# Transposes of seven late bursts on two engines, and another order of four readers of PSUM

## The chip, the cores and the metric

The kernel runs on one core of a Trainium2 chip. The metric is the device time of one execution in microseconds (us). The engines are TensorE (PE, with its weight loads PEld), VectorE (DVE), ScalarE (ACT), GpSimd (POOL) and SyncE (SP, which issues DMAs).

## The reference

Attention within chunks of 64 rows, over 8 batches, 8 heads and 576 rows of 64, then a feed-forward layer with softplus over the 4608 resulting rows:

```
scores = matmul(q_c, k_c^T) / sqrt(64)            # per chunk of 64 rows
attn   = exp(scores - max) ; attn /= sum(attn) + 1e-9
x      = (attn @ v_c), heads side by side          # 4608 x 512
h      = x @ w_in                                  # 512 x 2048
g      = max(h, 0) + log1p(exp(-|h|))              # softplus
out    = g @ w_out                                 # 2048 x 512
```

All in float32.

## The kernel before

**The work.** The rows are cut into 36 attention blocks of 128 rows (two chunks) and 9 row tiles of 512 rows for the feed-forward layer. Every float32 matrix product is made of three matmuls: a high part of each operand (rounded copy) and a low part (the difference), as high x high, low x high and high x low.

**The stages.** Row tiles 0 to 2 are done in the plain way, up to about 315 us. Then come three "super pairs" of two row tiles each. In a super pair the products with `w_in` are made in seven products P0 to P6 instead of eight, by sums of blocks; `pairs` holds eight steps of each super pair, called pairs here. In a pair, PE runs P1, P2, P0, P3, one product with `w_out` for the pair before (12 matmuls), P4, P5, P6, and another such product; then the next pair's P1. Each P has six matmuls. In the second half of super pairs 0 and 1 PE does only products with `w_out`. The third super pair (in `BOTH`) uses sums for `w_out` as well, so its pairs have two short products (`R1`, `R0`) of six matmuls there. 

**The banks.** `pa_tile()` gives a PSUM tile of two banks; there are two such tiles. In `product`, one tile holds banks 1 and 2 of the pair, the other banks 0 and 3. Readers of a pair: `hold` (s0, s1, s2) copies banks 0, 1, 2 out on ACT (L792). `mix` (L805) makes sums: `d` and `c22` on POOL, the others on DVE: `e` reads bank 3, `f` reads bank 1, `f2` reads bank 2, `c11` reads bank 0. `soft` (L816; L814 in the third super pair) applies softplus on ACT: `soft10` reads bank 1, `soft01` reads bank 2, `soft11` and `soft00` read sums in SBUF. The next pair's P1 takes the tile of banks 1 and 2, after `soft10`, `soft01` and `f2`.

**The bursts.** Attention of blocks 4 to 35 runs in bursts (`burst`): 64 small matmuls each for values and scores of two blocks. After a burst come, for each of its two blocks, maximum and subtraction (DVE), exp on ACT (with a table load of its own), the sum of exp (DVE), a normalization on DVE or POOL (L595), and the transposition of the exp values within each chunk, which the next burst needs as `eT`. The code uses VectorE's transpose on squares of 32x32 (`BL`), each transposed in its place. For blocks in `SWAP_DVE`, `blk_e4` makes eight transposes of a quarter of the partitions (L544): `Tf` is the first four, `Te` the other four. They read `qe` and write `eT`. For other blocks one whole transpose `blk_e` (L532) goes from `qe` to `ka`, and DMAs then move the squares across partitions. Blocks 22 to 35 belong to seven late bursts, in super pairs 0 and 1 (from about 357 us on). In super pairs 0 and 1 a burst stands in pairs 2, 5 and 7 and once in the second half.

**The order.** `Plan` decides the order of all instructions of each engine. It goes forward in time with a cost for each task, and starts on each free engine the ready task of lowest `urg` (then the one added first). A result counts as ready for another engine 0.15 us after its end (`CROSS`) and for the same engine 0.08 us after it (`OWN`). A task with `urg` of 0 or more isn't started when a task with negative `urg` on that engine is due within 0.5 us (`HOLD`). A change of ACT's function table between exp and softplus counts 1.28 us. The readers above have negative `urg`; the transposes have `urg=d`, which is positive. The order found is written out, the engines run their instructions in that order, and the waits between engines come from the framework, which tracks which tile is read and written.

Costs of the planner that matter here: P 1.36, product with `w_out` 2.72, `hold` 0.59, `mix` on DVE 0.69, softplus 0.60, normalization on DVE 0.65.

Of the kernel before, what the change touches and what calls it, by code (L numbers as in the profile page):

```python
# [33 lines left out]
class Plan:  # L34


    CROSS = 0.15
# [123 lines left out]
def chunked_attention_softplus_ffn(  # L161
# [9 lines left out]
    nc = tc.nc  # L171
# [4 lines left out]
    BL = 32  # L176
# [6 lines left out]
    NPT = B * NCH // 2  # L183
# [69 lines left out]
    live = {}  # L253
# [280 lines left out]
    def blk_et(i):  # L534
        return blk_tile("eT").rearrange("p (u h k) -> p u h k", u=2, h=H)

    def blk_e4(i, a):
# [7 lines left out]
        if a == 1:  # L545
            live.pop(("e", i)), live.pop(("eA", i))

    def blk_swap(i):
        ea = live.pop(("eA", i))
        eT = blk_et(i)  # L550
        for a in range(2):
            for kb in range(2):
                for tb in range(2):
                    d, s = (2 * a + kb) * BL, (2 * a + tb) * BL
                    (nc.scalar if i in SWAP_ACT else nc.sync).dma_start(eT[d : d + BL, tb], ea[s : s + BL, kb])
        live["eT", i] = eT
# [494 lines left out]
    WHOLE = (4, 5, 9)  # L1051
    SWAP_DVE = (4, 7, 9, 10, 11, 13, 14, 15, 16, 17, 19, 20, 21, 22, 23, 24, 25, 26, 27, 28, 29, 30, 31, 32, 33, 34, 35)
    SWAP_ACT = ()
    BEGIN = (4, 8, 15)
    BURST_AT = (22, 26, 32, 36, 40, 44)
    HOMES = {(n, i): ("early", 2 * (i - FIRST_BLK) + j) for i in (5, 7) for j, n in enumerate("qk")}
# [91 lines left out]
    for u, (g, is_in, fc) in enumerate(units):  # L1148
        (of_in if is_in else of_out)[fc] = u
        d = due(g) - 4  # L1150
        last = [f"w_hi{u}", f"w_lo{u}"]
        users = []
        if not is_in and fc >= HALF_FC:
            for j in range(2 * (fc - HALF_FC), min(2 * (fc - HALF_FC) + 2, LATE)):
# [11 lines left out]
                 urg=d, take=[("top", [f"w_add{u}"])])  # L1166
# [131 lines left out]
    for key, (pv, ps) in bursts.items():  # L1298
# [40 lines left out]
        for n in range(2):  # L1339
            i = a + n  # L1340
            plan.add(f"v{i}", LOADER.get(("v", i), "SP"), 2.4, partial(blk_v_load, i), free_of["v", i], urg=d + V_LATE if ("v", i) in HOMES else d - V_URG, kb=310, parts=4,
                     after=[V_AFTER])
            first = [f"B{at}_{n}"] if bursts[key][0] is None else [f"xh{2 * bursts[key][0] + n}"]
            plan.add(f"max{i}", "DVE", 0.68, partial(att_max, i), first, urg=d + 0.2 * n if key in BEGIN else n - 5,
                     after=[f"sub{a}"] if n else [])
            plan.add(f"sub{i}", "DVE", 0.68, partial(att_sub, i), [f"max{i}"], urg=d + 0.2 * n if key in BEGIN else n - 5)
            plan.add(f"exp{i}", "ACT", 0.62, partial(att_exp, i), [f"sub{b}"], urg=d if key in BEGIN else -6, table="exp",
                     after=[f"hi{at + 1}"] if at in BEGIN else [])
            plan.add(f"den{i}", "DVE", 1.25, partial(att_den, i), [f"exp{i}"], urg=d)
            pool = i in NORM_POOL  # L1350
            plan.add(f"norm{i}", "POOL" if pool else "DVE", 1.05 if pool else 0.65, partial(att_norm, i),
                     [f"den{i}"], urg=d)
            gone = [f"V{FIRST_BLK - 1}"] if ps == F else [f"B{at}_{n}"]
            if i in SWAP_DVE:
                plan.add(f"Tf{i}", "DVE", 1.76, partial(blk_e4, i, 0), [f"norm{i}"] + gone, urg=d)
                plan.add(f"Te{i}", "DVE", 1.76, partial(blk_e4, i, 1), [f"Tf{i}"], urg=d)
                swapped[i] = f"Te{i}"
            else:
                plan.add(f"Te{i}", "DVE", 0.65, partial(blk_e, i), [f"norm{i}"], urg=d)
                plan.add(f"swap{i}", "ACT" if i in SWAP_ACT else "SP", 4.8, partial(blk_swap, i), [f"Te{i}"] + gone, urg=d - SW_URG, kb=190, parts=8)  # L1360
                swapped[i] = f"swap{i}"
# [55 lines left out]
    for at, w in enumerate(pairs):  # L1417
        n, j, name = w["s"], w["j"], w["name"]
        d = due((n, 0, j)) - 9
        for part in range(2):  # L1420
            needs = [] if at > 1 else [f"G1_{FAST * FC - 1}"]
            if not at and not part:
                needs = [f"B{BURST_AT[-1]}_{i}" for i in range(2)]
            if n == 0:
                needs += [f"wd{j}_{i}" for i in range(3)] + own
            if n in BOTH and j % 2:
                needs += [f"x{q}{n}_{k}" for q in "HL" for k in range(7)]
            plan.add(f"ring{part}_{name}", QUEUE["ring"], ISSUE[QUEUE["ring"]], partial(ring_load, w, part), needs, urg=d - 20, kb=660 if part else 880,
                     take=[(("ring", "other")[n in BOTH and j % 2] + str(part), [f"P{6 if part else 3}_{name}"])] if at or part else [],
                     after=[f"ring{part}_{pairs[at - 1]['name']}"] if at else [])  # L1430
        for k in range(7):
            needs = [f"ring{k // NX}_{name}", f"xH{n}_{k}", f"xL{n}_{k}"]
            needs += [before[f"P{k}_{name}"]] + {4: [f"s1_{name}"], 5: [f"s2_{name}"], 6: [f"s0_{name}", f"e_{name}"]}.get(k, [])
            take = []
            if k == ORDER[0]:
                take = [("pa", [f"soft10_{name}", f"soft01_{name}", f"f2_{name}"])]
            elif k == ORDER[2]:
                take = [("pa", [f"c11_{name}", f"e_{name}"])]
            plan.add(f"P{k}_{name}", "PE", PM, partial(product, w, k), needs, urg=1e6, take=take)
        for q in range(3):  # L1440
            past = [f"{t}_{pairs[at - 1]['name']}" for t in (("soft11",), ("c22", "f"), ("d",))[q]] if at else []
            plan.add(f"s{q}_{name}", "ACT", 0.59, partial(hold, w, q), [f"P{q}_{name}"] + past, urg=-3 if n in BOTH else -2)
        for what, needs in (
            ("d", ["s1", "s2"]), ("e", ["s0", "P3"]), ("c22", ["e", "d"]), ("f", ["d", "P5"]), ("f2", ["f", "P5"]),
            ("c11", ["f2", "P6"]),
        ):
            pool = what in MIX_POOL
            past = [f"soft00_{pairs[at - 1]['name']}"] if at and what == "f" else []
            plan.add(f"{what}_{name}", "POOL" if pool else "DVE", 1.3 if pool else 0.69, partial(mix, w, what),
                     [f"{t}_{name}" for t in needs] + past, urg=-2)  # L1450
        a, b = (v_["name"] for v_ in w["first"])
        for i, jj, what in ((1, 0, "P5"), (0, 1, "P5"), (1, 1, "c22"), (0, 0, "c11")):
            kept = [f"lo{v_['name']}" for v_ in w["second"]] if j == FC // 2 - 1 else [f"us{name}"]
            take = {(1, 0): [("uu0", [f"lo{a}", f"lo{b}"])], (0, 1): [("uu1", kept)]}.get((i, jj), [])
            needs = [f"{what}_{name}"] + {(0, 0): [f"soft10_{name}"], (1, 1): [f"soft01_{name}"]}.get((i, jj), [])
            if n in BOTH:
                take = []
                if j > 1:
                    needs += [f"R{i}_{j - 2}", f"vt{j - 2}_{i}"] + [f"own{j - 2}{q}" for q in range(2)] * i
                elif j:  # L1460
                    needs += [f"B{tag(list(bursts)[-1])}_{b}" for b in range(2)]
                else:
                    needs += [f"lo{v_['name']}" for w_ in pairs[at - FC // 2 : at] for v_ in w_["second"]]
            plan.add(f"soft{i}{jj}_{name}", "ACT", 0.6, partial(soft, w, i, jj), needs, urg=-2, table="softplus", take=take)
        if n in BOTH:
            continue
        if j < FC // 2 - 1:
            plan.add(f"us{name}", QUEUE["us"], ISSUE[QUEUE["us"]], partial(spill_store, w), [f"soft01_{name}", f"soft11_{name}"], urg=-1, kb=400)
            a, b = (v_["name"] for v_ in w["second"])
            plan.add(f"ul{name}", QUEUE["ul"], ISSUE[QUEUE["ul"]], partial(spill_load, w), [f"us{name}", f"soft{1 - j % 2}{j % 2}_{n}_{FC // 2 - 1}"],  # L1470
                     urg=due((n, 1, 2 * j + 2)) - 12, kb=400,
                     take=[(f"uu{j % 2}", [f"lo{a}", f"lo{b}"])], after=[f"ul{n}_{j - 1}"] if j else [])
        for group in ("first", "second"):
            for i in (1, 0) if group == "first" else (0, 1):
                v_ = w[group][i]
                b = v_["name"]
                src = f"ul{name}" if group == "second" and j < FC // 2 - 1 else f"soft{i}{int(group == 'second')}_{name}"
                plan.add(f"hi{b}", "ACT", 0.62, partial(sp_hi, v_), [src], urg=-1, take=[("g", [f"G2_{b}"])],
                         after=[f"hi{w[group][1]['name']}"] if group == "first" and i == 0 else [])
                plan.add(f"lo{b}", "DVE", 0.69, partial(sp_lo, v_, False), [f"hi{b}"], urg=-1)  # L1480
# [198 lines left out]
```

## Time and profile before

| | |
|---|---|
| median of 3 runs | 832.38 us (832.22 to 832.39) |
| profiled execution, its own time | 831.0 us |
| its span, first to last instruction | 829.2 us |
| PE busy | 809.3 us, 98% of the span |
| DVE, ACT, POOL busy | 583.3, 403.1, 406.9 us |

The span is the profiled execution without what lies around it. Busy time is the union of an engine's instructions; waiting of the engine's sequencer isn't in it. Matmuls overlap, so the busy share of PE counts a pipelined stretch as full.

### The profile page before, as it was taken

Reading aid. Unit: us, or ns where it says so; the run is one execution under the profiler, and the core shown is the slowest. Engines: PE = TensorE matmul, PEld = TensorE weight load, DVE = VectorE, ACT = ScalarE, POOL = GpSimd, SP = SyncE. Lnnn points to the kernel's source line nnn. Section 1 sums busy time; section 2 is a strip of 40 time slices with the busy share of each in tenths; the row PEclk is TensorE's granted clock in tenths of the full one; section 3 lists DMA queues with packets and bytes.
Section 4 is the critical chain, followed back from the end, with each engine's and each line's share of the span. In section 5 each row is a group of like instructions: output and inputs, shape, how many; then the busy total and the mean of one; then the engine's idle time right before and its main releaser. Section 6 shows DMA issues by size and latency. Waiting matters only on the chain.

```text
span 829.2 us, 15528 instructions
## 1 busy us (share of the span) xinstructions
PE 809.3 (98%) x5675; PEld 664.0 (80%) x5675; DVE 583.3 (70%) x938; ACT 403.1 (49%) x664; POOL 406.9 (49%) x467
## 2 busy tenths in 40 slices
PE   8799999999999999999999999999999999999997
PEld 7688778888887888888888888888887787878886
DVE  4898987087478777667487888483878935555984
ACT  3767764345344564344434434434454644454551
POOL 1457659879975822322334212132188539972213
PEclk9899999999999999999999999999999999999999
DMA  9977758644674454776749536859558565666563
GB/s 207 251 181 201 188 174 238 199 111 123 152 199 112 112 145 153 226 214 180 205 164 225 151 105 205 230 162 233 158 149 269 190 228 187 208 218 212 158 208 68
DMA packets 202877, 151.27 MB, mean 182 GB/s; under 512 B 161136, under 2 KB 176752, under 8 KB 198576
## 3 DMA queue, kind: packets, MB, share of 16 engines
q1 hardware_dynamic: 189424, 99.66, 44.6%
q0 software_dynamic: 11232, 50.34, 19.8%
q8 instruction: 45, 0.74, 0.4%
q10 hardware_dynamic: 2144, 0.26, 0.2%
q14 instruction: 32, 0.26, 0.1%
HBM read 106.95 MB, written 41.94 MB: 180 GB/s over the span
## 4 chain that ended last, share of the span: by engine, by line
PE 74%; DVE 8%; DMA 5%; ACT 4%; POOL 3%; issue 3%; SPq 2%; DVEq 0%; POOLq 0%; ACTq 0%
PE po L1002 29%; PE pa L786 22%; PE pa L644 13%; PE po L938 8%; PE pa L608 2%; DVE wib L805 2%; PE pa L520 1%; DMA raw<-in_moe_w_in_dram 1%; DVE g_lo L660 1%; SPq L359 1%; POOL raw L873 1%; DMA images<-raw 1%; POOL wib L805 1%; DVE eT L544 1%; ACT ends L816 1%
## 5 line engine op out<-in xcount | busy, mean ns | idle before, releaser
L805 POOL TENSOR_TENSOR wib<-wib 128x512 f32<-128x512 f32 x48 | 65.5, 1364 | 180.7 <-ACT wib L792 158.5
L1002 PE MATMUL po<-late,g_hi 128*128 128x512 f32 x420 | 128.8, 392 | 0.0
L786 PE MATMUL pa<-wi_hi,xb 128*128 128x512 f32 x304 | 94.8, 393 | 1.8 <-DVE wib L805 1.1
L544 DVE STREAM_TRANSPOSE eT<-qe 32x256 f32<-32x256 f32 x216 | 93.9, 435 | 3.1
L1002 PEld LDWEIGHTS po<-late,g_hi 128*128 128x128 f32 x420 | 78.2, 188 | 16.6 <-DVE raw L1009 0.2
L1002 PE MATMUL po<-wo_hi,g_hi 128*128 128x512 f32 x224 | 85.2, 396 | 0.0
L786 PE MATMUL pa<-wib,xb 128*128 128x512 f32 x360 | 84.9, 389 | 0.0
L1002 PE MATMUL po<-wo_hi,g_lo 128*128 128x512 f32 x224 | 84.2, 392 | 0.6 <-DVE g_lo L660 0.6
L1002 PE MATMUL po<-wo_lo,g_hi 128*128 128x512 f32 x224 | 84.2, 392 | 0.0
L1002 PE MATMUL po<-late,g_lo 128*128 128x512 f32 x224 | 83.5, 390 | 0.3 <-DVE g_lo L660 0.3
L786 PEld LDWEIGHTS pa<-wib,xb 128*128 128x128 f32 x360 | 67.6, 188 | 14.1
L805 DVE TENSOR_TENSOR wib<-wib,pa 128x512 f32<-128x512 f32 x72 | 49.3, 685 | 36.6 <-ACT wib L792 21.9
L652 ACT ACTIVATE u<-pa 128x512 f32<-128x512 f32 (+1 forms) x50 | 29.0, 581 | 93.5 <-PE pa L644 91.6
L792 ACT COPY wib<-pa 128x512 f32<-128x512 f32 x72 | 40.5, 587 | 61.5 <-PE pa L786 61.5
L786 PEld LDWEIGHTS pa<-wi_hi,xb 128*128 128x128 f32 x304 | 56.5, 188 | 16.6 <-ACT ends L816 2.6
L660 DVE TENSOR_TENSOR g_lo<-ends,g_hi 128x512 fp32r<-128x512 f32 x64 | 49.4, 778 | 22.5 <-ACT g_hi L656 21.9
L656 ACT CAST g_hi<-ends 128x512 fp32r<-128x512 f32 x64 | 39.1, 618 | 46.4 <-PE po L1002 42.6
L786 PE MATMUL pa<-wi_lo,xb 128*128 128x512 f32 x152 | 59.2, 390 | 0.0
L746 POOL DMA_DIRECT2D xb<-scratch x39 | 22.1, 567 | 67.7 <-PE pa L786 52.4
L660 DVE TENSOR_TENSOR g_lo<-u,g_hi 128x512 fp32r<-128x512 f32 (+1 forms) x32 | 31.2, 976 | 30.0 <-ACT g_hi L656 24.3
L1002 PEld LDWEIGHTS po<-wo_hi,g_lo 128*128 128x128 f32 x224 | 42.4, 189 | 10.1 <-DVE g_lo L660 1.2
L805 DVE TENSOR_TENSOR wib<-pa,wib 128x512 f32<-128x512 f32 x24 | 16.6, 690 | 47.7 <-ACT ends L816 21.1
(288 smaller groups left out, 1831.0 us busy)
## 6 DMA issues: line engine op xcount, KB each, us to landing
xb<-scratch POOLq DMA_DIRECT2D x19, 1024.0 KB, 6.0
xb<-scratch POOLq DMA_DIRECT2D x20, 768.0 KB, 5.5
raw<-in_moe_w_in_dram SPq DMA_DIRECT2D x16, 512.0 KB, 5.3
raw<-in_moe_w_out_dram SPq DMA_DIRECT2D x16, 512.0 KB, 4.9
scratch<-ends SPq DMA_DIRECT2D x16, 512.0 KB, 3.1
out_dram<-raw SPq DMA_DIRECT2D x28, 256.0 KB, 4.0
spill<-ends SPq DMA_DIRECT2D x14, 512.0 KB, 3.9
ends<-spill SPq DMA_DIRECT2D x14, 512.0 KB, 4.1
```

What stands on the lines that cost most here:

```text
L544: nc.vector.transpose(live["eT", i][d : d + BL, tb], e[s : s + BL, kb])
L608: nc.tensor.matmul(pa[o, a, col : col + C], vt[r, 4 * j + 2 * h2 + c2, :], eT[r, :, 4 * c2 + 2 * j + h2, :], start=True, stop=True,)
L644: nc.tensor.matmul(ph, wt[:, c, :], x[:, ts_, c, :], start=(n == 0), stop=(n == 3 * KC - 1))
L652: nc.scalar.activation(w["u"], w["ph"], AF.Softplus)
L656: nc.scalar.copy(w["hi"], w["u"])
L660: (nc.gpsimd if pool else nc.vector).tensor_tensor(w["lo"], w["u"], w["hi"].bitcast(F32), op=ALU.subtract)
L746: on("ring").dma_start(t[:, : cols.stop - cols.start], src[:, cols])
L786: nc.tensor.matmul(w["bank"][BANK[k]], wts[:, q, c, :], x[:, c, :], start=k < NX and c + n == 0, stop=c == 1 and n == 2, skip_group_check= ...
L792: nc.scalar.copy(tmp_of(n), w["bank"][n])
L805: (nc.gpsimd if what in MIX_POOL else nc.vector).tensor_tensor(out, a, b, op=op)
L938: nc.tensor.matmul(live["acc", ACC[k]][ct][:, cols], (w[:, q] if k > 1 else w[q])[:, ct * P : (ct + 1) * P], g[:, cols], start=k < 3 and j ...
L1002: nc.tensor.matmul(pos[w["m"]][t], terms[n][0][:, j * P : (j + 1) * P], terms[n][1], start=(w["first"] and n == 0), stop=n == 2 and (w["la ...
```

## The change

For blocks 22 to 35 (`CROSS`) the eight quarter transposes are replaced. Two whole transposes (`blk_e2`) write the squares of 32x32, transposed in place, first to the block's `ka` tile (`eA`) and then to its `eT` tile. Then four copies (`blk_cross`), each of 32 partitions and 256 elements, bring the squares that lie off the diagonal of each chunk from `eA` to the right partitions of `eT`, on ACT. They are planned at 0.69 us for a transpose and 0.41 us for a copy, with the same `urg` as before.

Among the readers, `f2` now needs `soft01` instead of P5, `soft01` is added first and needs P5, `soft10` needs `f`, and `soft11` needs `soft10` instead of `soft01`.

```diff
+    def blk_e2(i, a):
+        e = live["e", i].rearrange("p a j (u k) -> p u (a j) k", u=2)
+        if a == 0:
+            nc.vector.transpose(live["eA", i], e)
+            return
+        live["eT", i] = blk_et(i)
+        nc.vector.transpose(live["eT", i], e)
+        live.pop(("e", i))
+
+    def blk_cross(i, n):
+        ea, eT = live["eA", i], live["eT", i]
+        a, kb = divmod(n, 2)
+        d, s = (2 * a + kb) * BL, (2 * a + 1 - kb) * BL
+        nc.scalar.copy(eT[d : d + BL, 1 - kb], ea[s : s + BL, kb])
...
+    CROSS = tuple(range(22, NPT))
+    CROSS_URG = 0
...
-            if i in SWAP_DVE:
+            if i in CROSS:
+                plan.add(f"Tf{i}", "DVE", 0.69, partial(blk_e2, i, 0), [f"norm{i}"] + gone, urg=d)
+                plan.add(f"Te{i}", "DVE", 0.69, partial(blk_e2, i, 1), [f"Tf{i}"], urg=d)
+                for n_ in range(4):
+                    plan.add(f"Tc{i}" + str(n_) * (n_ < 3), "ACT", 0.41, partial(blk_cross, i, n_),
+                             [f"Tc{i}{n_ - 1}" if n_ else f"Te{i}"], urg=d + CROSS_URG)
+                swapped[i] = f"Tc{i}"
+            elif i in SWAP_DVE:
                 plan.add(f"Tf{i}", "DVE", 1.76, partial(blk_e4, i, 0), [f"norm{i}"] + gone, urg=d)
...
-            ("d", ["s1", "s2"]), ("e", ["s0", "P3"]), ("c22", ["e", "d"]), ("f", ["d", "P5"]), ("f2", ["f", "P5"]),
+            ("d", ["s1", "s2"]), ("e", ["s0", "P3"]), ("c22", ["e", "d"]), ("f", ["d", "P5"]), ("f2", ["f", "soft01"]),
...
-        for i, jj, what in ((1, 0, "P5"), (0, 1, "P5"), (1, 1, "c22"), (0, 0, "c11")):
+        for i, jj, what in ((0, 1, "P5"), (1, 0, "f"), (1, 1, "c22"), (0, 0, "c11")):
...
-            needs = [f"{what}_{name}"] + {(0, 0): [f"soft10_{name}"], (1, 1): [f"soft01_{name}"]}.get((i, jj), [])
+            needs = [f"{what}_{name}"] + {(0, 0): [f"soft10_{name}"], (1, 1): [f"soft10_{name}"], (1, 0): [f"soft01_{name}"]}.get((i, jj), [])
```

## Rows read from the trace of the kernel before

**Rows 1.** The page: span, and PE's busy time, share of the span and instructions.

```profile
span 829.2 us, 15528 instructions
PE 809.3 (98%) x5675; PEld 664.0 (80%) x5675; DVE 583.3 (70%) x938; ACT 403.1 (49%) x664; POOL 406.9 (49%) x467
```

**Rows 2.** The waits of PE: who waited for whom, us in total, times, longest. Gaps under 0.15 us aren't in it.

```profile
PE pa L786 <- DVE wib L805: 1.4, 2, 1.1
...
PE po L1002 <- DVE g_lo L660: 0.9, 2, 0.6
```

**Rows 3.** Busy time by stage: the stretch, its length, then busy us (and instructions) of PE, PEld, DVE, ACT and POOL, the granted clock of PE, the DMA share and GB/s. Super pairs 0 and 1, then the pairs of the third.

```profile
315.00:660.00 345.00, 343.64 (x2392) 281.94 (x2391) 254.52 (x406) 155.73 (x256) 121.07 (x133) 1.00 0.67 192
660.00:765.00 105.00, 103.07 (x447) 83.04 (x446) 55.52 (x67) 47.88 (x91) 64.80 (x70) 1.00 0.61 204
```

**Rows 4.** The timeline of a pair of super pair 0 that follows a burst: start, duration, engine, line, operation, out<-in, shapes, count, idle time of the engine before it and who ended it. L792 is `s0`, the first L805 `e`, L595 the normalizations, POOL's L805 `d`, the 18 matmuls P4 to P6, L544 the quarter transposes, the first L816 `soft10`, then `f`, `f2` with `c11`, `soft01`, the last matmul before the next pair, and its P1.

```profile
414.97 0.62 PE L1002 MATMUL po<-late,g_hi 128*128 128x512 f32 x2
...
415.17 0.59 ACT L792 COPY wib<-pa 128x512 f32<-128x512 f32 x1 [1.56 <-PE pa L786]
...
415.79 0.69 DVE L805 TENSOR_TENSOR wib<-wib,pa 128x512 f32<-128x512 f32 x1 [0.56 <-ACT wib L792]
...
416.39 2.38 DVE L595 TENSOR_TENSOR qe<-qe,den 128x512 f32<-128x512 f32 x2
416.63 1.59 POOL L805 TENSOR_TENSOR wib<-wib 128x512 f32<-128x512 f32 x1 [0.63 <-DVE wib L805]
...
417.69 4.24 PE L786 MATMUL pa<-wib,xb 128*128 128x512 f32 x18
418.70 3.56 DVE L544 STREAM_TRANSPOSE eT<-qe 32x256 f32<-32x256 f32 x8
420.65 1.28 ACT L816 ACT_TABLE_LOAD   x1 [4.90 <-PE pa L786]
...
421.95 0.60 ACT L816 ACTIVATE ends<-pa 128x512 f32<-128x512 f32 x1
...
422.65 0.69 DVE L805 TENSOR_TENSOR wib<-pa,wib 128x512 f32<-128x512 f32 x1 [0.39 <-ACT ends L816]
...
423.37 1.48 DVE L805 TENSOR_TENSOR wib<-wib,pa 128x512 f32<-128x512 f32 x2
...
424.10 0.60 ACT L816 ACTIVATE ends<-pa 128x512 f32<-128x512 f32 x1 [1.55 <-DVE wib L805]
424.26 0.39 PE L1002 MATMUL po<-late,g_lo 128*128 128x512 f32 x1
424.75 0.73 PE L786 MATMUL pa<-wi_hi,xb 128*128 128x512 f32 x2
```

**Rows 5.** The same table load in three other pairs that follow a burst (timeline of ACT).

```profile
373.13 1.28 ACT L816 ACT_TABLE_LOAD   x1 [4.90 <-PE pa L786]
...
546.55 1.28 ACT L816 ACT_TABLE_LOAD   x1 [4.90 <-PE pa L786]
...
594.08 1.28 ACT L816 ACT_TABLE_LOAD   x1 [4.90 <-PE pa L786]
```

**Rows 6.** The timeline of two pairs of the third super pair. First the end of one and the next P1, then a whole reading of banks 1 and 2: a cast that stands ahead on ACT, `soft10`, `f`, `soft01`, `f2` with `c11`, and the next P1.

```profile
689.10 0.61 PE L938 MATMUL po<-g_lo,wo_hi 128*128 128x512 f32 x2
...
689.84 0.73 PE L786 MATMUL pa<-wi_hi,xb 128*128 128x512 f32 x2
...
738.54 0.41 ACT L877 CAST raw<-raw 128x256 fp32r<-128x256 f32 x1 [2.88 <-POOL raw L873]
...
738.85 0.59 ACT L814 ACTIVATE wo_hi<-pa 128x512 f32<-128x512 f32 x1
...
739.54 0.69 DVE L805 TENSOR_TENSOR wib<-pa,wib 128x512 f32<-128x512 f32 x1 [3.17 <-ACT wo_hi L814]
...
740.27 0.60 ACT L814 ACTIVATE wo_lo<-pa 128x512 f32<-128x512 f32 x1 [0.83 <-DVE wib L805]
...
740.90 1.48 DVE L805 TENSOR_TENSOR wib<-wib,pa 128x512 f32<-128x512 f32 x2 [0.66 <-ACT wo_lo L814]
...
741.64 0.74 PE L786 MATMUL pa<-wi_hi,xb 128*128 128x512 f32 x2 [1.06 <-DVE wib L805]
```

**Rows 7.** The timeline near the start, block 2: ACT copies one bank of a `pa` tile (L404), DVE the other (L408).

```profile
13.77 0.58 ACT L404 COPY late<-pa 128x512 f32<-128x512 f32 x1 [1.03 <-PE pa L398]
...
14.39 0.69 DVE L408 COPY late<-pa 128x512 f32<-128x512 f32 x1 [0.94 <-ACT late L404]
```

**Rows 8.** Durations: the quarter transposes from 280 to 660 us (count | busy us, mean ns), the whole transposes of other blocks (min/median/max ns, first and last start), and a cast of 256 elements a partition on ACT.

```profile
L544 DVE STREAM_TRANSPOSE eT<-qe 32x256 f32<-32x256 f32 x136 | 59.1, 434 | 1.9
...
L532 DVE STREAM_TRANSPOSE ka<-qe x5: 697/704/711, 71.5 to 284.0; 128x512 f32<-128x512 f32 x5
...
L877 ACT CAST raw<-raw 128x256 fp32r<-128x256 f32 x16 | 6.4, 406 | 7.5 <-POOL raw L873 7.5
```

**Rows 9.** The timeline in the second half of super pair 1: quarter transposes, a normalization and `g_lo` on DVE, and the matmul on PE that follows.

```profile
629.04 1.79 DVE L544 STREAM_TRANSPOSE eT<-qe 32x256 f32<-32x256 f32 x4
...
630.86 1.04 DVE L595 TENSOR_TENSOR qe<-qe,den 128x512 f32<-128x512 f32 x1
...
631.83 1.22 DVE L660 TENSOR_TENSOR g_lo<-ends,g_hi 128x512 fp32r<-128x512 f32 x1
...
633.11 0.50 PE L1002 MATMUL po<-wo_hi,g_lo 128*128 128x512 f32 x1 [0.60 <-DVE g_lo L660]
```

## The prediction

> **What bounds the kernel now.** I read the page first, to see which engine is full: TensorE (PE) is busy for 98% of the span [rows 1], so only its gaps can be given back. Then the waits of PE, to see who ends these gaps, and PE's busy time by stage, to see where they lie. The order of instructions, which is all that the change alters, can differ only from the first super pair on (from about 315 us). There PE is idle for 1.36 us of 345 and, in the last super, for 1.93 us of 105 [rows 3]. Two groups name the late party: the VectorE (DVE) combination at L805, and `g_lo` at L660, 0.9 us in two waits [rows 2]. The timeline of one pair with an activation table load [rows 4], and of one pair of the last super [rows 6], shows the rest: twelve times, five in the first two supers and seven in the last, the next pair's first product waits for the readers of the `pa` tile.
>
> One such stall costs more than its idle time. Matmuls of this shape start every 0.2265 us (18 of them in 4.24, the last lasting 0.39) [rows 4]. From 424.26 to 424.75 one start is 0.26 late, and the first two products then take 0.73 instead of 0.62: 0.37 us [rows 4]. The stall at 689.84 costs 0.28 + 0.11 = 0.39; that at 741.64, with 1.06 of idle time, 1.06 + 0.16 + 0.11 = 1.33 [rows 6].
>
> **Part one, the readers.** Removed: ScalarE (ACT) reading bank 1 (`soft10`) while DVE is meant to read bank 1 (`f`), then both bank 2 (`soft01`, `f2`). Put in: `soft01` and `f` first, on two banks, then `soft10` and `f2`. No operation is added. The store of the spilled halves on SP needs `soft11`, which now follows `soft10`: at most one reader (0.60) later, with its reload several pairs away. Today the four run strictly one after the other: 738.85, 739.54, 740.27, 740.90, then the product at 741.64, each starting 0.03 to 0.1 us after the one before ends [rows 6]. That `f` waits for `soft10` is one bank. That `soft01` (bank 2) waits for `f` (bank 1), 0.83 us of idle time ended by DVE, is not. Nor is it early in the kernel: DVE's copy out of one half of a `pa` tile starts at 14.39, when ACT's copy out of the other half ends (13.77 + 0.58 = 14.35), although both halves had been written before [rows 7]. So the kernel's waits follow the two-bank tile, not the bank, and the new order stays a chain of four. Its length: with `f2` right behind `f` on DVE (0.79 from start to start, as in the pair of 1.48 [rows 4]) and `soft10` last, 0.60 + 0.10 + 0.69 + 0.10 + 0.69 + 0.04 + 0.60 + 0.05 = 2.87 us, against 741.64 - 738.85 = 2.79 today [rows 6]. That adds 0.07 at six stalls of the last super: **+0.4**. After a table load the planner's costs (1.28 for it) put `soft10` ahead of `f2`, and the chain keeps today's 2.8.
>
> The Trainium skill (PSUM — Partial Sum Buffer, "PSUM bank collisions raise a hardware error") asks that engines be kept apart by bank and quadrant of 32 partitions only, so two readers of two banks could run together. By that rule this part would give -5.6 us (rival two) instead of +0.4; rows 6 and 7 speak for a wait by tile.
>
> **Part two, the transposes.** For 14 blocks, 8 quarter transposes at 0.434 us (3.5 us) become 2 whole ones; the nearest, of the same form of access, takes 0.704 [rows 8]. DVE saves 2.06 us a block, 29 in all. This is worth nothing in itself: in the pair with the table load `f` waits for ACT (0.39 <- ACT) after the transposes are over [rows 4]. One stall does hang on DVE's load: `g_lo` of 631.83 started behind four quarter transposes and a normalization, and PE waited until 633.11, 0.60 + 0.16 + 0.11 = 0.87 us [rows 9]. It goes away (-0.87) or stays (0), since ACT's casts wait there for other engines too; I take **-0.4**.
>
> ACT gets four copies of 32x256 a block, 56 in all. The trace has none of that shape; a 128x256 cast, as many elements a partition, takes 0.406 us [rows 8], so 1.6 us a block. ACT is busy for 45% of that stage [rows 3]; what counts is where in its queue they stand, for each waits for the second whole transpose, and everything behind it on ACT waits too.
>
> In the pair after a burst, ACT is empty for 4.90 us before the table load, in three pairs shown and a fourth alike [rows 4, 5]. I count from the end of P3: 414.97, 12 matmuls of 0.2265 (2.72 us) before P4 begins at 417.69; P5 ends after 12 more, at 5.44. The planner's own costs decide the order of issue, not the time: `e` from 0.15 to 0.84, two normalizations of 0.65 to 2.14, `Tf` of both blocks to 3.52 (the first block's `Te` is ready 0.08 too late to be picked before the second's `Tf`), `Te` of the first to 4.21. Then copies at 4.36 and 4.85, while `soft01` is due 0.15 after P5, at 5.59, and the hold of 0.5 shuts out a later one. So two copies are issued ahead of the table load of `soft01`.
>
> The chip is later than that. `e` starts at 415.79 (0.82), and the second normalization is stretched while GpSimd works: two take 2.38 us, from 416.39 to 418.77, with GpSimd busy from 416.63 for 1.59 [rows 4]. Three whole transposes from 418.70 end at 420.8, so the two copies run from 420.85 to 421.67, and the load that started at 420.65 starts 1.0 us later. With the first `Te` ahead of the second `Tf`, three copies would go from 420.15 to 421.4: 0.75 later. Bounds for one pair: 0 (no copy ahead of the load) and 1.85 (all four, 1.64 from 420.85); I take 0.85, between the two orders worked out. Nothing hides it: behind the load stand the four readers, and behind them the product, already 0.37 late. Four pairs (loads at 373.13, 420.65, 546.55, 594.08; the fifth, in the first pair of the next super, has its transposes around the load and is left at 0) give **+3.4**.
>
> Elsewhere a late copy is covered. In a pair without a load the readers are over 2.8 us after P5, and PE has P6 and 12 more matmuls, 6 x 0.2265 + 2.72 = 4.1 us: 1.3 to spare.
>
> **Sum**: 0.4 - 0.4 + 3.4 = +3.4 us. The profiled execution took 831.0 us, of which 829.2 is the span [rows 1]; the median of the runs is 832.38, so 1.4 longer. The sum goes on top of either: 834.4 for a profiled execution, **835.8** for the median. A difference under 0.2% (1.7 us) is about what a measurement of this kernel cannot tell from none.
>
> **Rivals.**
> One, the copies stay out of the way: they are issued behind the readers, or the second whole transpose is in time. For it: two tenths of a microsecond in the planner's bookkeeping move a copy to the other side of the hold. Against it: ACT is empty just there, so nothing keeps a ready copy back. Then +0.4 - 0.4 = 0: 832.4, no change. It decides at less than half a copy (0.4 us) a pair.
>
> Two, other side: readers of two banks do run together. Then `soft01` and `f` overlap, as do `soft10` and `f2`; the chain falls from 2.8 to about 1.5, and after a load further, since `f` no longer waits for it. All twelve stalls go: the idle time of both stages, 1.36 + 1.93, less the 0.9 of `g_lo`, is 2.4 [rows 2, 3], and 12 x 0.27 on top makes 5.6; the spare 1.0 hides the copies. 826.8. Against it stand rows 6 and 7. It decides if `f` starts before `soft01` ends.
>
> Three, other side as well: DVE's 29 us come back. Both `g_lo` stalls go, 0.9 + 2 x 0.27 = 1.4 [rows 2], and the casts that hold up `soft10` in the last super (one waited 2.88 for GpSimd until 738.54, [rows 6]) fall elsewhere: about 1.2 of the 1.33 there. With the copies harmless and the readers at +0.4: 832.4 - 2.2 = 830.2. It decides if both late `g_lo` are DVE's doing. Against it: DVE is not what these casts wait for.
>
> **How the numbers follow.** The copies ahead of the load: 0.52. Rival one: 0.25. Rival two: 0.07. Rival three: 0.13. The remaining 0.03 are three or four copies a pair, 838 and over. Of the first, about 0.03 fall under +1.7 (half the delay). Faster than 0.2%: 0.07 + 0.13 = 0.20. Within: 0.25 + 0.03 = 0.28. Slower: 0.49 + 0.03 = 0.52. The likeliest gives 835.8; by its own bounds (0.4 to 1.2 a pair, 633 at either end) 833.5 to 837.6. The range that leaves out no more than rival two and the far end takes in rivals one and three: 830.0 to 837.6.
>
> **What would show it.** Right: two copies from `ka` to `eT` on ACT right before the table loads near 374, 422, 548 and 595, the loads starting 0.7 to 1.0 us later after P5, and the product behind them with idle time of about 1 us instead of 0.1; `f` starting only when `soft01` ends; whole transposes near 0.70 and copies near 0.41. Wrong: loads still 0.2 us behind P5; or `f` beside `soft01`, with no idle time of PE at L786 in the last super; or copies that wait for DVE in the second halves, with PE then waiting for `g_lo`.

## The result, and the profile after

Timed side by side, the changed kernel took 834.54 us (median; 832.93 to 839.48) and the kernel before 831.15 us, a ratio of 1.0053 with a 95% interval of 1.0037 to 1.0069: slower by 0.5%. The profiled execution took 836.61 us (before 831.0), with a span of 834.7 us. From the first matmul of the first P1 to the last matmul of the last product with `w_in`, the only stretch in which the order of instructions differs, the two traces show 450.41 us (318.55 to 768.96) against 446.37 (317.38 to 763.75): +4.04 us. This stretch is used below for all kernels, since what precedes it varies from one execution to the next; each figure of it comes from one trace.

In the changed kernel the line numbers have moved: `hold` is L807, `mix` L820, the products L801, `soft` L831 (L829 in the third super pair), the normalizations L610, the whole transposes L551 and L554, the copies L561, `g_lo` L675, the `t_sum` subtractions L910, the weight-sum casts `v_hi` L892.

The page (as [rows 1]):

```profile
span 834.7 us, 15455 instructions
PE 809.7 (97%) x5675; PEld 663.9 (80%) x5675; DVE 555.4 (67%) x854; ACT 425.8 (51%) x720; POOL 409.8 (49%) x467
```

DVE lost 27.9 us of work and ACT gained 22.7. PE does the same 5675 matmuls in the same busy time, so the 4 us are gaps. The waits of PE (as [rows 2]; us in total, times, longest):

```profile
PE pa L801 <- DVE wib L820: 3.6, 4, 0.9
PE pa L801 <- ACT wo_hi L829: 3.0, 3, 1.1
PE po L1017 <- DVE g_lo L675: 2.7, 2, 1.8
```

Before, the first of these was 1.4 in two waits and the second wasn't there. (1.8 of the 2.7 lies at 201.69 us, before the changed stretch.) By stage (as [rows 3]): in super pairs 0 and 1 PE's idle time went from 1.36 to 4.49 us, in the third from 1.93 us of 105 to 3.35 of 106.

```profile
315.00:660.00 345.00, 340.51 (x2380) 279.81 (x2379) 219.54 (x319) 176.05 (x308) 122.21 (x133) 1.00 0.67 188
660.00:766.00 106.00, 102.65 (x445) 82.59 (x444) 57.32 (x67) 48.64 (x91) 65.01 (x70) 1.00 0.61 205
```

The pair of super pair 0 after a burst, the same one as [rows 4] (timeline):

```profile
416.89 0.61 PE L1017 MATMUL po<-late,g_hi 128*128 128x512 f32 x2
417.09 0.59 ACT L807 COPY wib<-pa 128x512 f32<-128x512 f32 x1 [1.57 <-PE pa L801]
...
420.62 1.29 DVE L551 STREAM_TRANSPOSE ka<-qe 128x512 f32<-128x512 f32 x2
421.84 1.26 DVE L554 STREAM_TRANSPOSE eT<-qe 128x512 f32<-128x512 f32 x2
422.53 0.82 ACT L561 COPY eT<-ka 32x256 f32<-32x256 f32 x2 [4.86 <-DVE eT L554]
...
423.37 1.28 ACT L831 ACT_TABLE_LOAD   x1
...
424.67 0.60 ACT L831 ACTIVATE ends<-pa 128x512 f32<-128x512 f32 x1
...
425.37 0.69 DVE L820 TENSOR_TENSOR wib<-pa,wib 128x512 f32<-128x512 f32 x1 [1.68 <-ACT ends L831]
...
426.09 0.60 ACT L831 ACTIVATE ends<-pa 128x512 f32<-128x512 f32 x1 [0.83 <-DVE wib L820]
...
426.72 1.48 DVE L820 TENSOR_TENSOR wib<-wib,pa 128x512 f32<-128x512 f32 x2
...
427.46 0.73 PE L801 MATMUL pa<-wi_hi,xb 128*128 128x512 f32 x2 [0.90 <-DVE wib L820]
```

Two copies stand between the second whole transpose and the table load. From the first matmul after P3 to the load it is 6.48 us, where [rows 4] have 420.65 - 414.97 = 5.68: the load starts 0.80 later. Behind it the four readers still run one after the other, and P1 finds 0.90 us of idle time. The same stall is at 379.14, 553.76 and 602.13.

The fifth table load, in the first pair of super pair 1, and the one of the third super pair went the other way. In these pairs ACT's timeline shows the load right behind the instruction before it:

```profile
496.73 1.06 ACT L786 CAST wib<-xa 128x1024 fp32r<-128x1024 f32 x1
497.80 1.28 ACT L831 ACT_TABLE_LOAD   x1
501.69 0.60 ACT L831 ACTIVATE ends<-pa 128x512 f32<-128x512 f32 x1 [2.60 <-PE pa L801]
...
672.25 1.28 ACT L829 ACT_TABLE_LOAD   x1
677.09 0.60 ACT L829 ACTIVATE ends<-pa 128x512 f32<-128x512 f32 x1 [3.55 <-PE pa L801]
```

Before, every one of these loads waited for P5, as those of [rows 4, 5] do ("<-PE pa"). Here the load runs in ACT's idle time, `soft01` alone waits for P5, and P1 of the next pair has no stall. The semaphores recorded in the traces say why: before, the first reader, `soft10`, waits for PE and for an earlier instruction of ACT, in all six pairs, and the wait for PE stands on the load ahead of it. The new first reader, `soft01`, has no wait for ACT and keeps its wait for PE on itself.

The third super pair (as [rows 6]; timelines of ACT, DVE and PE in the pair before 733 us):

```profile
730.13 0.41 ACT L892 CAST raw<-raw 128x256 fp32r<-128x256 f32 x1 [2.87 <-POOL raw L888]
730.44 0.59 ACT L829 ACTIVATE wo_lo<-pa 128x512 f32<-128x512 f32 x1
...
732.58 0.60 ACT L829 ACTIVATE wo_hi<-pa 128x512 f32<-128x512 f32 x1 [1.55 <-DVE wib L820]
...
731.13 0.69 DVE L820 TENSOR_TENSOR wib<-pa,wib 128x512 f32<-128x512 f32 x1 [3.17 <-ACT wo_lo L829]
731.86 1.48 DVE L820 TENSOR_TENSOR wib<-wib,pa 128x512 f32<-128x512 f32 x2
...
733.23 0.73 PE L801 MATMUL pa<-wi_hi,xa 128*128 128x512 f32 x2 [1.06 <-ACT wo_hi L829]
```

`soft01`, `f`, `f2`, `soft10`, P1: 733.23 - 730.44 = 2.79 us, as before. But a cast that waited 2.87 us for GpSimd stands ahead of the first reader here, and again in the next pair (1.06 at 746.82); before, one pair had that ([rows 6], 738.54). In the pair before 707 us two subtractions stand ahead of `f` on DVE, and PE waits 0.88 us at 706.92:

```profile
702.66 1.11 DVE L910 TENSOR_TENSOR eT<-eT 128x512 f32<-128x512 f32 x1
703.80 1.11 DVE L910 TENSOR_TENSOR eT<-qe,eT 128x512 f32<-128x512 f32 x1
```

With the prediction's cost of a stall (idle time + 0.16 + 0.11), the bill is, in super pairs 0 and 1: four stalls of 0.90 instead of 0.10, +3.2; the fifth gone, -0.4; `g_lo` near 633 and 659 gone (0.60 and 0.30 of idle time), -1.4, and one of 0.89 at 652.25 new, +1.2. In the third: the load's stall gone, -0.4; two stalls of 0.88 and 1.06 where 0.12 and 0.31 were, +1.5. Together +3.7 of the 4.04.

### The profile page after: what moved, and what is told of

Same layout as the page of the kernel before. It is cut to its first block, busy times and chain, and to the rows that moved or that the text cites. A ratio compares the mean times of both kernels' runs of the same rounds, so it can differ in the third digit from the quotient of the medians.

```text
span 834.7 us, 15455 instructions
## 1 busy us (share of the span) xinstructions
PE 809.7 (97%) x5675; PEld 663.9 (80%) x5675; DVE 555.4 (67%) x854; ACT 425.8 (51%) x720; POOL 409.8 (49%) x467
## 4 chain that ended last, share of the span: by engine, by line
PE 79%; DVE 9%; ACT 4%; SPq 2%; DMA 2%; issue 2%; POOL 1%; DVEq 0%; POOLq 0%; ACTq 0%
PE po L1017 32%; PE pa L801 23%; PE pa L659 13%; PE po L953 8%; DVE wib L820 2%; PE pa L623 2%; SPq L359 2%; PE pa L520 2%; DMA raw<-in_moe_w_in_dram 1%; DVE g_lo L675 1%; DVE qe L610 1%; DVE qe L507 1%; ACT L831 1%; ACT ends L831 1%; DVE ka L551 0%
## 5 line engine op out<-in xcount | busy, mean ns | idle before, releaser
L820 POOL TENSOR_TENSOR wib<-wib 128x512 f32<-128x512 f32 x48 | 64.7, 1347 | 187.4 <-ACT wib L807 167.8
L801 PE MATMUL pa<-wi_hi,xb 128*128 128x512 f32 x304 | 94.6, 392 | 4.9 <-DVE wib L820 3.6
L801 PE MATMUL pa<-wib,xb 128*128 128x512 f32 x360 | 84.8, 389 | 0.0
L801 PEld LDWEIGHTS pa<-wib,xb 128*128 128x128 f32 x360 | 67.6, 188 | 14.0
L675 DVE TENSOR_TENSOR g_lo<-ends,g_hi 128x512 fp32r<-128x512 f32 x64 | 48.3, 756 | 38.1 <-ACT g_hi L671 38.1
L801 PEld LDWEIGHTS pa<-wi_hi,xb 128*128 128x128 f32 x304 | 56.5, 188 | 19.3 <-DVE wib L820 5.3
L807 ACT COPY wib<-pa 128x512 f32<-128x512 f32 x72 | 41.1, 587 | 60.2 <-PE pa L801 60.2
L820 DVE TENSOR_TENSOR wib<-wib,pa 128x512 f32<-128x512 f32 x72 | 49.4, 685 | 29.7 <-ACT wib L807 25.7
L801 PE MATMUL pa<-wi_lo,xb 128*128 128x512 f32 x152 | 59.2, 390 | 0.0
L675 DVE TENSOR_TENSOR g_lo<-u,g_hi 128x512 fp32r<-128x512 f32 (+1 forms) x32 | 34.8, 1087 | 29.8 <-ACT g_hi L671 24.0
L1017 PEld LDWEIGHTS po<-late,g_lo 128*128 128x128 f32 x224 | 42.0, 188 | 11.8 <-DVE g_lo L675 3.2
L1017 PEld LDWEIGHTS po<-wo_lo,g_hi 128*128 128x128 f32 x224 | 42.4, 189 | 8.8
```

Of the source, the lines that this page charges most:

```text
L675: (nc.gpsimd if pool else nc.vector).tensor_tensor(w["lo"], w["u"], w["hi"].bitcast(F32), op=ALU.subtract)
L801: nc.tensor.matmul(w["bank"][BANK[k]], wts[:, q, c, :], x[:, c, :], start=k < NX and c + n == 0, stop=c == 1 and n == 2, skip_group_check= ...
L807: nc.scalar.copy(tmp_of(n), w["bank"][n])
L820: (nc.gpsimd if what in MIX_POOL else nc.vector).tensor_tensor(out, a, b, op=op)
L1017: nc.tensor.matmul(pos[w["m"]][t], terms[n][0][:, j * P : (j + 1) * P], terms[n][1], start=(w["first"] and n == 0), stop=n == 2 and (w["la ...
```

## The experiments

**The theory and its rivals.** A: the copies ahead of a table load delay the load, and all behind it, by their length; the new order frees the load of its wait for P5. B: readers of two banks gain or lose by themselves, whatever the copies do. C: what counts is DVE's shorter work. (Each expectation states a theory A and rivals of its own; up to the doubled copies, its A is the one given here.) The runs take each part alone, move the copies, double them, and free the tiles.

**The readers' order alone.** The kernel before with the readers' part of the diff and none of the transposes' part:

```
-("f2", ["f", "P5"]),            +("f2", ["f", "soft01"]),
-((1, 0, "P5"), (0, 1, "P5"),    +((0, 1, "P5"), (1, 0, "f"),   (and the needs of soft11 and soft10)
```

> The kernel before with the new order of the readers alone. Theory A (the copies ahead of the table load make the loss, and the new order frees the load): soft01 carries one wait, so the load no longer waits for P5 and starts some 3 to 5 us earlier, in ACT's idle time; six stalls of 0.37 us go, 2.2 us faster, ratio 0.997. The four readers stay one after the other, 2.8 us from the first reader to the next P1. Theory B (the order of the readers makes the loss, by 0.07 us a pair or by what it moves in the last super): 0.5 to 1.5 us slower, ratio 1.001 to 1.002. Theory C (two banks side by side): f starts with soft01, no idle time of PE at the products of the last super, ratio 0.993.

835.54 us, ratio 1.0053 (1.0032 to 1.0075); 451.69 us in the changed stretch, +5.3. A had foreseen a gain, and was wrong. ACT's and DVE's timelines of the pair, and its P1:

```profile
415.24 1.28 ACT L816 ACT_TABLE_LOAD   x1
420.07 0.60 ACT L816 ACTIVATE ends<-pa 128x512 f32<-128x512 f32 x1 [3.55 <-PE pa L786]
...
418.16 3.55 DVE L544 STREAM_TRANSPOSE eT<-qe 32x256 f32<-32x256 f32 x8
421.75 0.69 DVE L805 TENSOR_TENSOR wib<-pa,wib 128x512 f32<-128x512 f32 x1
422.47 1.79 DVE L544 STREAM_TRANSPOSE eT<-qe 32x256 f32<-32x256 f32 x4
424.29 1.48 DVE L805 TENSOR_TENSOR wib<-wib,pa 128x512 f32<-128x512 f32 x2
...
425.03 0.73 PE L786 MATMUL pa<-wi_hi,xb 128*128 128x512 f32 x2 [0.92 <-DVE wib L805]
```

The load is freed as A says: it starts at 415.24, and `soft01` is done at 420.67. But `f` stands behind eight quarter transposes until 421.75, and the planner, which expects the load in front of `soft01`, has put four more (1.79 us) between `f` and `f2`. The gain is spent on DVE, and the stall is 0.92 to 0.95 at all five loads of super pairs 0 and 1. So here DVE's work did set the end, which A had left out. In the third super pair the load's stall is gone, and three P1 wait 0.89, 1.06 and 1.06 us as in the changed kernel: that loss comes with the order of the readers, whatever the transposes.

**The transposes and copies alone.** The changed kernel with the old order of the readers:

```
-("f2", ["f", "soft01"]),        +("f2", ["f", "P5"]),
-((0, 1, "P5"), (1, 0, "f"),     +((1, 0, "P5"), (0, 1, "P5"),   (and the old needs)
```

> The kernel before with the new transposes and copies alone, the old order of the readers. Theory A: two copies stand ahead of the table load in four pairs, each load starts 0.8 us later after the end of P3 than before, each of the four products behind 0.8 us later: 3.2 us, less up to 0.9 for the g_lo stall near 633; 2.3 to 3.5 us slower, ratio 1.003 to 1.004. Theory B: no loss here, ratio 0.999 to 1.000.

833.62 us, ratio 1.0036 (1.002 to 1.0052); +3.4 in the stretch (449.73). As A foresaw. ACT's timeline, and a line of the waits of PE:

```profile
420.75 0.82 ACT L561 COPY eT<-ka 32x256 f32<-32x256 f32 x2 [4.86 <-DVE eT L554]
421.60 1.28 ACT L831 ACT_TABLE_LOAD   x1
```

```profile
PE pa L801 <- ACT ends L831: 3.6, 4, 0.9
```

The same two copies, the same four stalls of 0.9. The two parts by themselves give +5.3 and +3.4, together +4.0: the parts don't add, for the whole transposes take away the quarter transposes that cost the first part its gain, and the copies then delay the load that it had freed.

**The copies held back.** The changed kernel, with the first copy of each block after the bursts of pairs 2 and 5 (and so all its copies) ordered behind `soft10` of the next pair:

```
 plan.add(f"Tc{i}" + ..., "ACT", 0.41, ..., urg=d + CROSS_URG,
+         after=[f"soft10_{key[0]}_{key[2] + 1}"] if not n_ and not key[1] and key[2] < FC // 2 - 1 else [])
```

> The changed kernel, with the first copy of a block held back until soft10 of the pair after its burst is issued (bursts of pairs 2 and 5 of super pairs 0 and 1), so that no copy stands ahead of the table load there. Nothing else is altered. Theory A: the four stalls of 0.90 us idle time at the products go altogether, because the load can then start in ACT's idle time: 4 x 1.17 = 4.7 us less than the changed kernel, so about 0.5 us faster than the kernel before, ratio 0.997 to 1.000. Theory B (the loss lies in the last super and at g_lo): as the changed kernel, ratio 1.004 to 1.006.

828.18 us, ratio 0.9979 (0.9963 to 0.9994): faster than the kernel before, with the same instructions on every engine as in the changed kernel. The pair's timeline:

```profile
414.51 1.28 ACT L831 ACT_TABLE_LOAD   x1
...
419.34 0.60 ACT L831 ACTIVATE ends<-pa 128x512 f32<-128x512 f32 x1 [3.55 <-PE pa L801]
...
421.75 1.48 DVE L820 TENSOR_TENSOR wib<-wib,pa 128x512 f32<-128x512 f32 x2
...
423.22 0.62 PE L801 MATMUL pa<-wi_hi,xb 128*128 128x512 f32 x2
```

`f` starts at 420.44 (behind a transpose of `q`) and `soft10` at 421.12. All five stalls of super pairs 0 and 1 are gone. Against the changed kernel the stretch is 4.8 us shorter (445.65): the place of the copies in ACT's order is worth more than the whole loss. Against the kernel before it is 0.7 us shorter; the three stalls of the third super pair are still there (0.89, 1.07, 1.07).

**The copies held back under the old order.** As above, on the transposes' part alone (behind `soft01`, which is the later of the two readers there).

> The transposes' and copies' part alone, under the old order of the readers, with the copies after the bursts of pairs 2 and 5 held behind soft01 of the next pair. Theory A (two separate effects: the copies ahead of a table load cost their length, and the new order of the readers frees the load of its wait for P5; shorter work on VectorE is worth nothing here by itself): the loads wait for P5 as in the kernel before, the stalls at the five table-load pairs are 0.37 us again, the one near 633 us goes, and the time is that of the kernel before, a ratio of 0.999 to 1.001; against the changed kernel with the copies behind soft10 it lacks some 2 us. Rival (the gain of the copies held back comes from VectorE's shorter queue, not from the order of the readers): the stalls at the table loads go here too and the ratio is 0.997 to 0.998.

830.44 us, ratio 0.9992 (0.9979 to 1.0006). As A foresaw, and against C. ACT's timeline:

```profile
419.70 1.28 ACT L831 ACT_TABLE_LOAD   x1 [4.90 <-PE pa L801]
```

The load waits for P5 again, and P1's idle time is 0.09 at all five loads, as before. DVE's shorter work alone changes nothing that can be measured. Against the copies held back under the new order this run lacks 1.0 us in the stretch, not the 2 that A expected, for the third super pair takes part of that order's gain. This run and the four above make the table of the stretch, in us:

| | quarter transposes | copies ahead of the load | copies held back |
|---|---|---|---|
| old order of readers | 446.37 | 449.73 | 446.66 |
| new order | 451.69 | 450.41 | 445.65 |

**The copies doubled.** The changed kernel, with the first two copies of blocks 22, 24, 30 and 32 made twice:

```
+for _ in range(2 if n < 2 and i in TWICE else 1):
     nc.scalar.copy(eT[d : d + BL, 1 - kb], ea[s : s + BL, kb])
```

> The changed kernel with the first two quarter copies of the first block made twice, in the four bursts whose copies stand ahead of soft01's table load: two more copies of about 0.41 us ahead of each of the four loads, nothing else moved. Theory A (every copy ahead of the load delays the load, soft01, f, soft10, f2 and the next P1 by its own length): the four stalls at P1 grow from about 0.9 to about 1.7 us, the time rises by 4 x 0.82 = 3.3 us over the changed kernel, a ratio to the kernel before of about 1.009. Rival (the copies cost because they wait for VectorE's whole transposes or because ScalarE is busier, not by standing ahead of the load): the stalls stay near 0.9 us and the ratio near 1.005.

ACT's timeline and the P1 behind it:

```profile
427.95 1.70 ACT L562 COPY eT<-ka 32x256 f32<-32x256 f32 x4 [4.86 <-DVE eT L554]
429.66 1.28 ACT L832 ACT_TABLE_LOAD   x1
...
433.75 0.73 PE L802 MATMUL pa<-wi_hi,xb 128*128 128x512 f32 x2 [1.77 <-DVE wib L821]
```

Four stalls of 1.77 (7.1 in all) instead of 0.90: 0.87 for 0.88 us more of copies (1.70 - 0.82). The changed stretch took 453.81 us, 3.4 more than in the changed kernel, as A foresaw. The whole time did not follow: 843.83 us, ratio 1.015 (1.0121 to 1.0179), with executions from 837.32 to 845.59. The profiled one had lost another 4.5 us before the first P1 (at 323.08, against 318.55), where the order of instructions is not changed. The trace shows where: DVE waited 1.81 us for a DMA of `q` at 108.49, PE then waited 1.85 us for DVE (until 115.63), and behind that the granted clock of PE was 0.50 (1.2 GHz) for 3.41 us (busy time by stage):

```profile
116.93:120.34 3.41, 3.41 (x10) 2.67 (x9) 3.31 (x7) 2.21 (x5) 1.33 (x2) 0.50 0.01 2
```

Eight matmuls started 0.43 us apart there instead of 0.23, which is 1.6 us; waits of 0.84 and 0.40 us followed at 130.60 and 131.71. Why the DMA was late, and whether the other executions lost their time in the same way, stays open.

**The quarter transposes kept out of the readers' way.** The readers' order alone, with the quarter transposes after the bursts of pairs 2 and 5 ordered behind `f2` of the next pair.

> The readers' part alone, with the quarter transposes after the bursts of pairs 2 and 5 held behind f2 of the next pair. Theory A (the readers' part alone lost its time because quarter transposes stood on VectorE ahead of f and between f and f2): the stalls of about 0.92 us at four of the five table-load pairs go to nothing, the one at the first pair of the second super step and those of the last super step stay, so some 4 us less than the readers alone, a ratio to the kernel before of 0.998 to 1.001. Rival (the new order of the readers is itself the longer chain at a table load): the stalls stay near 0.9 us and the ratio near 1.005.

839.69 us, ratio 1.0119 (1.0101 to 1.0137): slower still, and neither side's number. The four stalls did go, as A said; DVE's timeline behind `f2` of one of these pairs (422.27) and two lines of PE's waits show what came instead:

```profile
423.67 1.77 DVE L544 STREAM_TRANSPOSE eT<-qe 32x256 f32<-32x256 f32 x4
...
426.76 3.59 DVE L544 STREAM_TRANSPOSE eT<-qe 32x256 f32<-32x256 f32 x8
...
431.10 1.80 DVE L544 STREAM_TRANSPOSE eT<-qe 32x256 f32<-32x256 f32 x4
```

```profile
PE po L1002 <- DVE g_lo L660: 5.0, 4, 1.7
...
PE pa L520 <- DVE ka L497: 2.0, 3, 1.4
```

7.2 us of transposes, moved behind `f2`, run into the next pair; the transposes of `q` and `k` (L497) for the next burst come late (1.40 at 614.37), and so do three `g_lo` (1.54, 1.20 and 0.58; the fourth, at 200.59, lies before the changed stretch). In the third super pair four P1 waited 1.05 to 1.37 us. In neither of the two places tried do the quarter transposes suit the new order; whole transposes with the copies held back do.

**Two tiles for the banks.** The readers' order alone, with banks 1 and 3 on one PSUM tile and banks 2 and 0 on the other:

```
-if k in (ORDER[0], ORDER[2]):  ... {1: t[:, 0], 2: t[:, 1]} if k == 1 else {0: t[:, 0], 3: t[:, 1]}
+if k in (ORDER[0], ORDER[1]):  ... {1: t[:, 0], 3: t[:, 1]} if k == 1 else {2: t[:, 0], 0: t[:, 1]}
```

> As the first kernel of this call (new order of the readers, old transposes), but banks 1 and 3 share one PSUM tile and banks 2 and 0 the other, so that f and soft01, and soft10 and f2, read different tiles. If the waits go by tile: f starts with soft01 (0.1 us apart instead of 0.7), soft10 with f2, the next P1 is released about 1.5 us after the first reader instead of 2.8, the stalls at the products of the last super go, but for what a late first reader leaves: 4 to 5.6 us faster than the kernel before, ratio 0.993 to 0.996. If two readers on ACT and DVE cannot run side by side for another reason: as the first kernel of this call.

DVE's and ACT's timelines of the pair, then DVE's and PE's near 700 us:

```profile
419.83 0.69 DVE L805 TENSOR_TENSOR wib<-pa,wib 128x512 f32<-128x512 f32 x1
420.06 1.16 ACT L816 ACTIVATE ends<-pa 128x512 f32<-128x512 f32 x2 [5.78 <-PE pa L786]
...
696.78 5.08 DVE L895 TENSOR_TENSOR eT<-eT 128x512 f32<-128x512 f32 x1
...
703.60 0.68 DVE L805 TENSOR_TENSOR wib<-pa,wib 128x512 f32<-128x512 f32 x1
...
704.97 0.72 PE L786 MATMUL pa<-wi_hi,xa 128*128 128x512 f32 x2 [3.34 <-ACT wo_hi L814]
```

`f` of 419.83 and `soft01` of 420.06 run at the same time, on two banks in two tiles; in no trace with both banks in one tile do they. So the readers of two banks were kept apart by the tile and not by the banks, and the prediction's reading of [rows 6, 7] holds. That agrees with the Trainium skill (PSUM — Partial Sum Buffer, "PSUM bank collisions raise a hardware error"), which asks engines to be kept apart by bank and partition quadrant only.

The time was 837.35 us, ratio 1.0081 (1.006 to 1.0102), and not the gain expected (453.07 us in the stretch): the stalls behind the loads went, but in the third super pair P1 or P4 waited 1.21, 3.34, 1.67 and 1.20 us, for `e` now holds up P4 on the same tile and `f` stands behind subtractions that took 5.08 and 1.78 us. Behind the wait of 3.34 us the granted clock was 0.50 for 3.41 us (from 706.45), which costs 1.6 us more. So what the two tiles are worth by themselves is not shown.

**The third super pair.** Two ways to take back its loss, both on the copies held back. First the old order of the readers in the third super pair alone.

> The changed kernel with the copies behind soft10 and with the old order of the readers in the last super step alone. Theory A (the last super step has no table load to free, so there the new order gains nothing and only moves casts and t_sums ahead of the readers): the last super step's stalls are those of the kernel before again (one of about 1.06 us where there are three), some 1.2 us less than the copies behind alone, a ratio of 0.995 to 0.997. Rival (the new order gains about 0.1 us at each pair there): no less than the copies behind alone, 0.998 or more.

828.01 us, ratio 0.9974 (0.996 to 0.9987), 444.65 us in the stretch. PE waits at a P1 there for 0.31 and 1.06 us, as before [rows 2, 6], where the copies held back have 0.89, 1.07 and 1.07. In the stretch that is 1.0 us less than the copies held back; in the whole time the two can't be told apart, and the ratio lies between the two that were expected. Second, casts and subtractions ordered not at all in the last 1.0 us ahead of a reader:

```
-... <= now + self.HOLD
+... <= now + (self.HOLD_V if t["name"][:2] in ("vh", "ts") else self.HOLD)     (HOLD_V = 1.0)
```

> The changed kernel with the copies behind soft10 and, in addition, the weight-sum casts (line 892) and the t_sum subtractions kept out of the last 1.0 us ahead of a reader that the order expects (0.5 us for all else). Theory A (the last super step loses about 1 us at each pair where a cast or a t_sum stands ahead of the first reader and waits for GpSimd): up to three stalls of 0.9 to 1.1 us go, 1 to 3 us less than the copies behind alone, a ratio of 0.994 to 0.997. Rival (those stalls come from the new chain itself): they stay, ratio 0.998.

840.24 us, ratio 1.0143 (1.0119 to 1.0167), 455.22 us in the stretch: a miss. The stalls did not go: one P1 waited 2.55 us at 748.35, behind a subtraction that started at 742.32 and took 4.02 us, and the granted clock was 0.50 for 3.41 us from 748.54; another waited 1.97 at 705.03. Four `g_lo` came late as well (0.48 to 1.49). The old order there takes the stalls back; this hold of 1.0 us does not keep these casts and subtractions out of the way.

## Why the prediction was right, and where it wasn't

The sign and the size came out: predicted +3.4 us for the kernel, measured 834.54 - 831.15 = 3.4 between the medians, and 4.0 in the changed stretch of the traces. The main term, the copies, was right by its mechanism. That the sum fits so closely is in part luck: the readers' term came out as +0.8 (-0.7 at two loads and +1.5 in the third super pair) where +0.4 stood for another reason, and 0.3 of the 4.0 is not accounted for.

**The copies ahead of the load (+3.4 predicted).** Right in number, place and size: two copies in each of four pairs, 0.82 us for two, the load 0.80 later (predicted 0.75 to 1.0), four stalls of 0.90, 4 x 0.80 = 3.2 us more than before. Three whole transposes, from 420.62 to 422.5, stand ahead of the copies, as worked out. The run with the copies doubled gives the slope: 0.87 for 0.88.

**The waits follow the tile.** Right; the two-tile run shows the other case.

**The readers (+0.4 predicted).** The step that failed. The chain in the third super pair was put at 2.87 us; it is 2.79. The term was mis-sized by taking 0.79 from `f` to `f2` out of a pair of 1.48, where they start 0.73 apart (731.13, 731.86). And the step "after a table load the chain keeps today's 2.8" left out what stands before the chain: the load itself. In the kernel before it waited for P5, since the wait of `soft10` for PE stood on it; with `soft01` first it doesn't. That is worth 0.4 at each load where no copy is in the way, the two loads of first pairs here (-0.7), all six once the copies are held back. The sentence that took "[4.90 <- PE]" at the load as given was where it could have been seen: what waits for P5 is the reader, and the load itself can run before P5 has ended (415.24 in the readers' order alone).

**The third super pair.** Not foreseen: the new order moves one of ACT's casts ahead of the first reader in one pair more, and two subtractions of 1.11 us each ahead of `f` in another, +1.5. The readers' order alone shows the same stalls, and the old order there takes them back.

**`g_lo` (-0.4 predicted).** The stall near 633 went, and so did the one near 659; another of 0.89 us came at 652.25. Together -0.3 us, the number for another reason.

**"Worth nothing in itself."** DVE's 29 us are worth nothing under the old order (ratio 0.9992). Under the new order they decide: 451.69 us in the stretch with quarter transposes, 445.65 without and the copies held back. Rival one ("copies out of the way": no change) was too low in its gain: with the copies behind the readers the kernel is faster by 0.2%, since the freed load then shows.

## What to carry to other kernels

Ask of every table load which wait stands on it: if the first instruction behind it has more than one, the load may wait for data that it doesn't need, and another instruction ahead in the order can free it. Work that is moved to an idle engine is not free there: find the instruction with a deadline that stands behind it, and order the moved work behind that one. An edit that loses alone (here the readers' order, +5.3 us in the stretch) and one that is worth nothing alone (the transposes with their copies held back, +0.3) can be a gain together (-0.7), and the place in the queues can decide the sign, so measure them apart and together.

## What the runs showed of the hardware that was not expected

A subtraction of two 128x512 tiles on DVE (`t_sum`) takes 0.67 to 0.70 us wherever no tensor operation of GpSimd runs beside it, 236 times in the eleven traces. All the longer ones have one beside them for at least half of their time: 1.11 twice in a row (702.66 and 703.80 in the changed kernel), and in two runs 5.08 and 4.02 us (696.78 with two tiles, 742.32 with the casts held), while GpSimd ran one tensor operation after another. But 33 that had one beside them took no longer than alone. The normalizations show the same: 0.65 to 0.69 us alone, and 2.38 for two with GpSimd busy beside them. That GpSimd is the cause is argued from these coincidences and not tested.

In three of the traces the granted clock of PE fell from 1.00 to 0.50 for 3.41 us in the middle of the kernel, each time behind a long wait of PE (1.85, 2.55 and 3.34 us; the copies doubled, the casts held, two tiles). Each fall cost 1.6 us beyond the wait (eight matmuls 0.43 us apart instead of 0.23).

A copy of 32x256 on ACT takes 0.40 us (0.401 to 0.408 for the 56 of the changed kernel), as long as a cast of 128x256 [rows 8]: a quarter of the partitions saves nothing.
